# Moving a corner of the first weight split and the denominator product from VectorE to GpSimd in a fused mLSTM and two-MLP kernel

## Chip, cores and metric

The kernel runs on one core of a Trainium2 chip. The metric is the device time of one execution in microseconds (us); the time quoted for a kernel is the median of its runs.

## What is computed

Three stages in float32. First an mLSTM recurrence over 768 steps for 2 batches and 8 heads of 40 features, with input, forget and output gates. Its output, 1536 tokens of 320 features, goes through a gated MLP (two input matrices of 320x1536, an output matrix of 1536x320) and then through a SiLU MLP (320x2048 and 2048x320).

```python
for t in range(S):
    m_new = np.maximum(f_gate[:, :, t] + m, i_gate[:, :, t])
    f_stab, i_stab = np.exp(f_gate[:, :, t] + m - m_new), np.exp(i_gate[:, :, t] - m_new)
    C = f_stab * C + i_stab * outer(v, k)
    n = f_stab * n + i_stab * k
    y[:, :, t] = sigmoid(o_gate[:, :, t]) * (C @ q) / np.maximum(np.abs(n @ q), 1.0)
x = y.transpose(0, 2, 1, 3).reshape(B * S, H * D)
x = (x @ w_a) * (x @ w_b) @ w_out
h = x @ w_in
out = (h * (1.0 / (1.0 + np.exp(-h)))) @ w_out2
```

## The kernel before

**Units.** The recurrence is computed in chunks of 128 steps. A unit u (0 to 11) is one chunk of one batch, so 128 tokens. Of each unit TensorE makes the scores (`s_u`), the values (`y_u` from `vx_u` and `e_u`), the part carried over from earlier chunks (`y_u` from `cn_u`) and the update of the state (`ups_u`). VectorE scans the decays into `e_u` (line 396), multiplies the scores by them (line 425), joins the values (474, 476) and makes the unit's output `x_u` in `outputs()`: the absolute value of the denominator, its maximum with 1, the reciprocal `dn_u`, the product y times `dn_u` (line 486) and the product with the output gate (line 488). The sigmoid of the output gate stands in place in the third part of `kvo_u`, the tile that holds k, v and o of the unit; two such tiles alternate. `x_u` is transposed on TensorE (`px_u`, line 515) and stored as a high and a low part in `xring` (ScalarE line 518, VectorE line 231).

**Weights.** The first MLP has 12 blocks j of 128 hidden features. `load_w1` brings each as two raw tiles. `split_w1(j, 1)` and `split_w1(j, 0)` turn a raw tile into a tile `cvt_j` (ScalarE lines 237 and 241, VectorE line 245), round it into the high part of `w_j` (ScalarE lines 257, 264, 266) and subtract to get the low part (`rest`, line 231). Two `cvt` tiles alternate between all these parts, so the first step of a part waits until the part two before it has been read for the last time. The last 64 of the 320 input features share one 128-row slab: their high part stands in one half of the partitions and their low part in the other half, so the subtraction of the low part (64x128, twice a block) writes to other partitions than it reads.

**Stages.** The first MLP works in passes over blocks of 2 or 3 units and ranges of j (`PASSES`): `m0` is units 0 and 1 with j 0 to 4, `m1` units 2 and 3, and so on; in a pass, `a` and `b` are the two products of the first layer (`h`, line 537), `c` the second layer (`acc`, lines 546 to 548). The second MLP begins inside the last pass (`n0`) and then runs alone.

**Order.** All the work up to the first block of the second MLP is cut into steps, and the table `ORDER` names which step is recorded next; each engine carries out its instructions in that order. `warm` is 8 small matmuls on the tile `idle` whose result nothing reads (line 367). All DMAs of the kernel are issued from the queue of SyncE (SP), in the order of the table too; an issue that waits for a buffer holds back the ones behind it.

Of the kernel before, what the change touches and what calls it, by code (L numbers as in the profile page):

```python
# [48 lines left out]
u4.out u4.upd w6.b m1.1.a lw8 u5.d0 w7.a u5.sk u4.out w7.a m1.0.b u3.upd u9.f1 m1.1.b l6.k l5.t w7.b m0.4.b m1.2.a
w7.a m1.2.b l6.t m1.0.b m1.1.b u4.adv w7.b w7.b m1.0.b u5.s0 w8.b w7.a m0.4.c u5.s1 u5.w0 m1.2.a m1.3.a u5.sv u3.adv  # L50
u5.w1 u5.v0 u5.f1 l6.q u5.car w8.b w8.b m1.1.b u4.d1 m1.2.b m1.0.b u5.v1 l6.k l7.k m1.3.a m1.3.b w8.b u5.comb u5.sk
u4.px w7.b l6.e lw9 m0.end m0.end m1.4.a u5.sig w8.a m1.1.b w8.a l7.k l6.k u7.f1 lw10 l7.k w8.b u5.out m1.0.c w7.b
u5.out u5.upd u4.xs l7.e m1.1.c m1.3.b u5.px m1.2.b w9.a m1.4.a u5.xs w7.b m1.4.b w8.a u5.adv m1.3.b w8.b l7.q m1.2.b
m1.2.c w8.a u6.s1 u6.s0 u4.xs w8.a u5.xs m2.0.a u6.car m2.1.a w9.b m1.3.b m1.4.b m1.3.c m2.0.a u0.comb m2.0.b u6.sv
l8.q m1.4.b m2.1.b u6.d0 m1.4.b w9.a w9.a m2.0.b m2.2.a u6.sk u6.sig m1.4.c m2.1.a u6.w0 m1.end m2.2.a m1.end m2.2.b
u10.sk m2.1.b w9.a m2.0.b u6.v0 w9.a m2.1.b m2.0.b u6.w1 u7.s0 m2.3.a u6.sk m2.1.b m2.0.c l8.k l8.k m2.4.a w9.b l8.k
m2.3.b w10.b m2.2.b u7.d0 m2.2.b m2.4.b w9.b m2.3.a lw11 l8.e u6.v1 l7.t m2.3.b m2.4.a m2.1.c u7.sk m3.5.a u7.w0
m2.2.b l8.t l9.e m2.3.b m3.5.a u7.s1 m2.3.b m2.4.b m2.4.b u6.comb m3.5.b m2.2.c m3.6.a m4.5.a u9.d1 m3.6.a m2.3.c
m3.6.b m3.5.b w10.b l9.t u8.s1 u8.f0 u6.out l9.q m3.7.a w10.b u6.upd w9.b m4.5.a m2.4.b u8.d0 w9.b m3.7.a m3.7.b l9.k
l9.k u11.f0 m3.6.b m2.4.c m3.5.b m3.7.b m4.6.a m4.5.b m2.end w10.a m3.6.b u11.sk w10.a u7.sk u7.sv m3.5.b u8.sk u8.s0  # L60
u7.w1 m3.5.c w10.b u2.f1 u6.adv m2.end u5.d1 m4.6.b w9.b m4.6.a m3.6.b m4.5.b m4.7.a m3.7.b m3.7.b m4.7.b l10.q m4.6.b
m5.5.a m3.6.c m3.7.c u6.out u8.sv m4.7.a m5.5.a u7.v0 w10.b u8.w1 u7.v1 m4.5.b w11.b u7.car m4.7.b w11.b m3.end m3.end
w10.b m4.6.b m4.5.b m5.6.a m4.7.b w10.a l9.k m4.5.c m5.5.b m4.6.b u8.w0 u7.sig m4.6.c w11.b u7.comb m4.7.b m5.6.a
m4.7.c u7.out m5.5.b m5.6.b m5.6.b m5.7.a u8.car m5.5.b m6.8.a w10.a m6.8.b m5.7.a u7.out u7.d1 w11.b u8.v0 u8.sk
m6.9.a m6.8.a m4.end u8.sig m6.8.b m4.end m5.7.b w11.a m5.6.b m5.5.b u7.upd m5.7.b l10.k m5.5.c m5.7.b w10.a m5.6.b
m6.9.a u9.d0 u8.v1 m6.8.b m5.6.c w11.a m6.10.a l10.k w11.b m6.10.a m6.9.b u8.comb m6.8.b w11.a w11.b m6.10.b m5.7.b
u9.sk m6.9.b w11.a l10.e m7.8.a u6.px m5.7.c u9.f0 w11.a m6.9.b u7.adv m6.10.b u9.sk m7.8.a l10.k m6.10.b m6.11.a
m6.8.c m6.9.b m6.10.b l10.t u8.upd m6.11.a u8.out u9.s1 m7.8.b m6.11.b m6.9.c u6.xs m5.end u9.sig m5.end u6.xs m6.11.b
u8.out m6.10.c m7.9.a m7.8.b u9.s0 l11.k u8.adv m7.9.b m7.10.a u8.px m6.11.b m6.11.b m7.8.b m7.8.b m7.10.b u7.px l11.k
u9.sv m7.9.a m7.10.a m7.11.a u9.w1 m6.11.c m7.11.b u10.sv m7.9.b m7.11.a m7.10.b m8.8.a u10.s0 l11.q m7.8.c u10.d0  # L70
u7.xs l11.t m7.9.b m7.9.b m6.end m8.8.b m7.10.b u9.w0 m8.9.a u6.f0 m8.8.a m7.9.c m8.9.b m7.11.b m8.9.a u7.xs m6.end
m8.8.b u8.xs u9.car u8.xs u9.upd u9.v0 m7.10.b m8.10.a u10.w0 l11.e m7.11.b m8.9.b m7.10.c u4.f0 m7.11.b m7.11.c l11.k
m8.9.b m8.8.b u9.v1 u9.adv u10.d1 m7.end u10.car u10.s1 m8.11.a u9.comb m8.10.b m8.10.a u10.w1 m8.11.b m9.0.a u9.out
# [735 lines left out]
```

## Time and profile before

| | us |
|---|---|
| median of 3 runs | 477.45 (473.94 to 478.1) |
| the profiled execution | 473.43 |
| its span, from the first to the last instruction | 471.7 |
| TensorE busy in the span | 458.2 (97%) |
| VectorE busy | 210.6 (45%) |
| ScalarE busy | 208.1 (44%) |
| GpSimd busy | 169.4 (36%) |

The profiled execution has its own time, 1.73 us more than its span. Every duration further down is from that execution, so a sum made of them stands against 473.43. The mean granted TensorE clock was 0.994 of full speed. In the table of stages each engine has its busy time and, in brackets, its number of instructions. PEld is TensorE's weight load, DVE VectorE, ACT ScalarE, POOL GpSimd.

### The profile page before, as it was taken

To read this page: it belongs to the slowest core of one execution; us is meant where nothing else is said; L and a number is where in the kernel's file an instruction comes from. 1 tells how busy PE (TensorE), PEld (TensorE's weight loads), DVE (VectorE), ACT (ScalarE), POOL (GpSimd) and SP (SyncE) were. 2 spreads that over 40 slices of the span, in tenths; PEclk is the share of its full clock that TensorE was granted. 3 is DMA by queue.
4 is the path that set the end of the run, shared out by engine and by line. 5 is a ranking of instruction groups with operands and counts; after the bars stand their busy time and mean duration, and the time that the engine had idled before them with its cause. 6 is when DMAs were issued, how large, how long until landed. Compare 5 with 4: busy or idle time off the path is not lost.

```text
span 471.7 us, 7975 instructions
## 1 busy us (share of the span) xinstructions
PE 458.2 (97%) x3095; PEld 438.3 (93%) x3095; DVE 210.6 (45%) x406; ACT 208.1 (44%) x461; POOL 169.4 (36%) x187
## 2 busy tenths in 40 slices
PE   6988999999999999999999999999999999999996
PEld 5988999999999999999999999998999998999995
DVE  7799997746547554523444574375420000000000
ACT  3676466444443321222355546565444233343333
POOL 2654635553344313112122223334342433433332
...
GB/s 242 227 230 247 309 137 245 187 79 92 21 26 154 49 18 91 63 2 61 17 166 65 107 127 75 123 75 109 1 0 57 0 1 1 1 56 1 0 1 56
DMA packets 14289, 41.52 MB, mean 88 GB/s; under 512 B 1772, under 2 KB 6284, under 8 KB 14252
## 3 DMA queue, kind: packets, MB, share of 16 engines
...
q14 instruction: 13, 0.11, 0.1%
...
## 4 chain that ended last, share of the span: by engine, by line
PE 87%; DVE 7%; ACT 2%; issue 2%; DMA 1%; SPq 0%; ACTq 0%; DVEq 0%
PE h L537 46%; PE acc L546 8%; PE acc L547 8%; PE acc L548 8%; PE s_u L418 3%; PE y_u L431 3%; PE cw L546 2%; PE cw L547 2%; PE cw L548 2%; DVE e_u L396 2%; PE px_u L515 2%; PE y_u L441 1%; PE fb_u L387 1%; DVE cvt_j L245 1%; PE ups_u L451 1%
## 5 line engine op out<-in xcount | busy, mean ns | idle before, releaser
L537 PE MATMUL h<-xring,w_j 128*128 128x256 f32 (+2 forms) x1088 | 184.6, 318 | 0.5 <-DVE g L588 0.5
L537 PEld LDWEIGHTS h<-xring,w_j 128*128 128x128 f32 x1088 | 162.3, 189 | 5.0 <-DVE g L588 0.7
L231 POOL TENSOR_TENSOR g<-g,g 128x256 fp32r<-128x256 f32 (+1 forms) x60 | 56.0, 935 | 147.0 <-ACT g L557 141.4
L231 POOL TENSOR_TENSOR g2w<-gw,g2w 128x512 fp32r<-128x512 f32 x48 | 63.3, 1319 | 110.9 <-ACT g2w L557 108.8
L537 PE MATMUL h<-xeven,w_j 128*128 128x512 f32 x256 | 64.0, 392 | 0.0
L537 PEld LDWEIGHTS h<-xeven,w_j 128*128 128x128 f32 x256 | 47.0, 188 | 8.5
L588 DVE TENSOR_TENSOR g<-a,h 128x256 f32<-128x256 f32 (+1 forms) x60 | 28.1, 471 | 58.2 <-POOL g L231 28.0
L594 ACT ACTIVATE gw<-h 128x512 f32<-128x512 f32 x48 | 28.7, 597 | 57.2 <-PE h L537 54.6
L557 ACT CAST g<-g 128x256 fp32r<-128x256 f32 (+1 forms) x60 | 26.8, 449 | 60.8 <-PE acc L548 32.3
L231 DVE TENSOR_TENSOR w_j<-cvt_j,w_j 64x128 fp32r<-64x128 f32 (+2 forms) x72 | 34.5, 479 | 29.4 <-ACT w_j L286 17.1
L581 ACT ACTIVATE a<-h 128x256 f32<-128x256 f32 (+1 forms) x60 | 25.5, 425 | 48.8 <-PE h L537 39.8
L546 PE MATMUL acc<-w_j,g2w 128*128 128x320 f32 x144 | 44.2, 310 | 0.0
L547 PE MATMUL acc<-w_j,g2w 128*128 128x320 f32 x144 | 44.0, 309 | 0.0
L557 ACT CAST g2w<-gw 128x512 fp32r<-128x512 f32 x48 | 29.8, 622 | 30.5 <-PE acc L548 30.1
L548 PE MATMUL acc<-w_j,g2w 128*128 128x320 f32 x144 | 39.9, 311 | 0.0
L546 PE MATMUL acc<-w_j,g 128*128 128x320 f32 x120 | 38.5, 321 | 0.7 <-DVE x L616 0.3
L548 PE MATMUL acc<-w_j,g 128*128 128x320 f32 x120 | 37.1, 309 | 0.0
L547 PE MATMUL acc<-w_j,g 128*128 128x320 f32 x120 | 37.0, 308 | 0.0
L231 POOL TENSOR_TENSOR w_j<-cvt_j,w_j 128x320 fp32r<-128x320 f32 (+1 forms) x24 | 26.3, 1100 | 26.6 <-ACT w_j L257 15.1
L546 PEld LDWEIGHTS acc<-w_j,g2w 128*128 128x128 f32 x144 | 27.1, 188 | 1.4
L547 PEld LDWEIGHTS acc<-w_j,g2w 128*128 128x128 f32 x144 | 27.1, 188 | 1.4
L548 PEld LDWEIGHTS acc<-w_j,g2w 128*128 128x128 f32 x144 | 26.4, 188 | 0.6
(109 smaller groups left out, 667.1 us busy)
## 6 DMA issues: line engine op xcount, KB each, us to landing
...
```

The source lines that it names most:

```text
L231: return eng.tensor_tensor(out=out_, in0=x, in1=hi.bitcast(F32), op=ALU.subtract)
L396: nc.vector.tensor_tensor_scan(out=e, data0=f, data1=ident8[:, h].rearrange("p h t -> p (h t)"), initial=0.0, op0=ALU.mult, op1=ALU.add)
L418: nc.tensor.matmul(out=s[:, i], lhsT=kz[u % 2][:, j, g], rhs=un["q", u][:, g], start=True, stop=True)
L431: nc.tensor.matmul(out=T["y1"][:, h], lhsT=un["e", u][:, h], rhs=T["v"][:, h], start=True, stop=True)
L537: nc.tensor.matmul(out=po, lhsT=w[:, wi * P:(wi + 1) * P], rhs=xt[:, :, xi], start=(n == 0), stop=(n == len(pairs) - 1))
L546: nc.tensor.matmul(out=o, lhsT=hi, rhs=w[:, off:off + DM], start=first, stop=False)
L547: nc.tensor.matmul(out=o, lhsT=hi, rhs=w[:, off + DM:off + 2 * DM], start=False, stop=False)
L548: nc.tensor.matmul(out=o, lhsT=lo, rhs=w[:, off:off + DM], start=False, stop=last)
L557: nc.scalar.copy(out=t[:, 0], in_=g)
L581: nc.scalar.activation(out=a[j], in_=pa, func=ACT.Copy, scale=WS ** -2)
L588: nc.vector.tensor_tensor(out=g, in0=a.pop(j), in1=pb, op=ALU.mult)
L594: nc.scalar.activation(out=g, in_=ph, func=ACT.Silu, scale=1 / WS)
```

## The change

Three edits.

1. In `split_w1(j, 1)` the low part of the last 64 features is no longer subtracted by VectorE into the other half of the partitions. GpSimd subtracts it, in two halves of 64x128, into a new tile `tl` (two of them alternate) in the partitions in which it reads, and two DMAs on SP's queue carry the halves into their place in `w_j`.
2. In `outputs()` VectorE no longer multiplies y by `dn_u`. GpSimd multiplies the output gate by `dn_u` in place, and VectorE's last product takes that.
3. `ORDER` is another table throughout: the steps of the new pieces are in it (59 more entries in all), one `warm` is gone, and nearly all others stand at other places.

```diff
@@ ORDER
-const l1.q const u3.f0 li const const zeros lf run0 u3.f1 warm lw0 run0 l0.t u6.d1 warm expf0 l0.k l0.k run1 run1
+lf const zeros zeros const const const li l0.q warm const run0 lw0 l0.k l0.k l0.t run0 run0 warm expf0 run1 sel run1
...
@@ split_w1, part 1
         yield
+        tl = cvt.tile([P, P], F32R, tag="tl", name=f"tl_j{j}")
         for p, q_, s_ in halves[::-1]:
-            rest(nc.vector, t[q_, s_], c[p, 0:P], t[p, s_])
-        yield
+            rest(nc.gpsimd, tl[p], c[p, 0:P], t[p, s_])
+            yield
+        for p, q_, s_ in halves[::-1]:
+            nc.sync.dma_start(out=t[q_, s_].bitcast(F32), in_=tl[p].bitcast(F32))
+            yield
         rest(nc.gpsimd, t[:, 10 * P + DM:], c[:, P:], t[:, 10 * P:10 * P + DM])
@@ outputs
             nc.vector.reciprocal(out=dn, in_=d)
-            nc.vector.tensor_tensor(out=y, in0=y, in1=dn.to_broadcast([P, H, D]), op=ALU.mult)
+            yield
+            od = un["o", u]
+            nc.gpsimd.tensor_tensor(out=od, in0=od, in1=dn.to_broadcast([P, H, D]), op=ALU.mult)
+            yield
             T["x"] = x = at.tile([P, 3 * P], F32, tag="x", name=f"x_u{u}")
             nc.vector.tensor_tensor(out=x[:, 0:DM].rearrange("p (h d) -> p h d", d=D), in0=y,
-                                    in1=un["o", u], op=ALU.mult)
+                                    in1=od, op=ALU.mult)
             yield
```

What the table does on three engines is shown at the start of the program, where units 0 and 1 are brought to their outputs. Lines 231, 245, 488 and 515 of before are lines 234, 248, 498 and 525 of the kernel after; line 486 has no counterpart, line 495 is the new product on GpSimd and line 276 the new DMA.

VectorE before, from the conversion of the block j 3 to the output of unit 1 (`cvt_j3` is that block's converted tile, `x_u1` the output):

```order
L245 SCALAR_TENSOR_TENSOR cvt_j3_432<-cvt_j3_432,cw_444 128x448
L396 SCALAR_TENSOR_TENSOR e_u2_437<-e_u2_437,ident8_93 128x1024
L360 COPY gb_97<-pgb_474 120x36
L245 SCALAR_TENSOR_TENSOR cvt_j3_446<-cvt_j3_446,cw_464 128x512
L231 TENSOR_TENSOR w1_j3_431<-cvt_j3_432,w1_j3_431 64x128 x2
L482 TENSOR_SCALAR y1_u1_425<-y1_u1_425 128x8
L483 TENSOR_SCALAR y1_u1_425<-y1_u1_425 128x8
L485 RECIPROCAL dn_u1_508<-y1_u1_425 128x8
L486 TENSOR_TENSOR y1_u1_425<-y1_u1_425,dn_u1_508 128x8x40
L488 TENSOR_TENSOR x_u1_511<-y1_u1_425,kvo_u1_254 128x320
```

VectorE after, the same place:

```order
L403 SCALAR_TENSOR_TENSOR e_u2_386<-e_u2_386,ident8_93 128x1024
L248 SCALAR_TENSOR_TENSOR cvt_j3_447<-cvt_j3_447,cw_461 128x448
L489 TENSOR_SCALAR y1_u1_453<-y1_u1_453 128x8
L490 TENSOR_SCALAR y1_u1_453<-y1_u1_453 128x8
L492 RECIPROCAL dn_u1_492<-y1_u1_453 128x8
L498 TENSOR_TENSOR x_u1_503<-y1_u1_453,kvo_u1_291 128x320
L367 COPY gb_97<-pgb_474 120x36
L248 SCALAR_TENSOR_TENSOR cvt_j3_499<-cvt_j3_499,cw_518 128x512
L432 TENSOR_TENSOR e_u2_386<-s_u2_509,e_u2_386 128x512
```

The two rows of line 231 and the two of line 486 are gone from ahead of `x_u1` (of line 231 there were 8 instructions in all up to there), and the second conversion of j 3 (`cvt_j3_446`, now `cvt_j3_499`) stands behind it.

TensorE before, from the transposes of unit 1 to the first products of the first MLP (`h`; `ups` is the update of the state, `y2` the carried part):

```order
L515 MATMUL px1_u1_539<-ident_90,x_u1_511 128x128 x3
L451 MATMUL ups_u1_543<-vx_u1_372,kvo_u1_254 120x123 x3
L441 MATMUL y2_u2_552<-cn_u0_411,qT_u2_462 128x123 x2
L441 MATMUL y2_u2_552<-cn_u0_411,qT_u2_462 128x82
L537 MATMUL h_568<-xring_91,w1_j0_184 128x256 x8
L537 MATMUL h_581<-xring_91,w1_j0_184 128x256 x8
L431 MATMUL y1_u2_593<-vx_u2_560,e_u2_437 128x41 x4
L537 MATMUL h_599<-xring_91,w1_j1_276 128x256 x8
L451 MATMUL ups_u2_608<-vx_u2_560,kvo_u2_514 120x123 x3
```

TensorE after, from the last of the 8 warm matmuls that stand behind the transposes of unit 1 (`s_u2` is the second half of the scores of unit 2):

```order
L374 LDWEIGHTS idb_92
L374 MATMUL idle_113<-idb_92 128x128
L458 MATMUL ups_u1_547<-vx_u1_326,kvo_u1_291 120x123 x3
L425 MATMUL s_u2_557<-qT_u2_342,kz0_108 128x128 x4
L547 MATMUL h_569<-xring_91,w1_j0_209 128x256 x8
L547 MATMUL h_583<-xring_91,w1_j0_209 128x256 x8
L438 MATMUL y1_u2_597<-vx_u2_530,e_u2_386 128x41 x8
L547 MATMUL h_611<-xring_91,w1_j1_273 128x256 x8
L448 MATMUL y2_u2_624<-cn_u0_443,qT_u2_342 128x123 x2
L448 MATMUL y2_u2_624<-cn_u0_443,qT_u2_342 128x82
L547 MATMUL h_637<-xring_91,w1_j1_273 128x256 x8
```

The 8 warm matmuls and the second half of the scores now stand ahead of the first `h`, and the carried part `y2_u2` stands behind three of them; before, the scores of unit 2 stood ahead of `px1_u1`.

GpSimd before, around the low parts of the blocks j 2 and j 3 and up to unit 2:

```order
L231 TENSOR_TENSOR w1_j2_337<-cvt_j2_338,w1_j2_337 128x320
L231 TENSOR_TENSOR w1_j2_337<-cvt_j2_382,w1_j2_337 128x512
L231 TENSOR_TENSOR w1_j3_431<-cvt_j3_432,w1_j3_431 128x320
L231 TENSOR_TENSOR w1_j3_431<-cvt_j3_446,w1_j3_431 128x512
L401 COPY vx_u2_560<-isg_96 128x8
L402 TENSOR_TENSOR vx_u2_560<-kvo_u2_514,isg_96 128x8x40
```

GpSimd after, the same place (`dn_u0` and `dn_u1` are the reciprocals of units 0 and 1):

```order
L234 TENSOR_TENSOR tl_j2_441<-cvt_j2_354,w1_j2_353 64x128
L495 TENSOR_TENSOR kvo_u0_145<-kvo_u0_145,dn_u0_401 128x320
L234 TENSOR_TENSOR tl_j2_441<-cvt_j2_354,w1_j2_353 64x128
L417 TENSOR_TENSOR kvo_u1_291<-kvo_u1_291,ec_u1_344 128x320
L662 COPY scratch_110<-ident_90 16x120
L234 TENSOR_TENSOR w1_j2_353<-cvt_j2_354,w1_j2_353 128x320
L234 TENSOR_TENSOR w1_j2_353<-cvt_j2_384,w1_j2_353 128x512
L495 TENSOR_TENSOR kvo_u1_291<-kvo_u1_291,dn_u1_492 128x320
L234 TENSOR_TENSOR tl_j3_501<-cvt_j3_447,w1_j3_446 64x128 x2
L408 COPY vx_u2_530<-isg_96 128x8
L409 TENSOR_TENSOR vx_u2_530<-kvo_u2_408,isg_96 128x8x40
L234 TENSOR_TENSOR w1_j3_446<-cvt_j3_447,w1_j3_446 128x320
```

The products with `dn_u0` and `dn_u1` and the halves in `tl` now stand between the low parts of the weights; that of `dn_u1` is directly behind the 128x512 low part of j 2.

SP's queue before, from the load of the raw block j 3:

```order
L206 DMA raw1_j3_363<-in_w1_dram 128x1024
L206 DMA raw1_j3_365<-in_w1_dram 128x896
L196 DMA e_u2_437<-fsd_98 128x1024
L184 DMA kz0_108<-in_k_cols_dram 40x384
L174 DMA qT_u2_462<-in_q_cols_dram 120x384
L206 DMA raw1_j4_492<-in_w1_dram 128x1024
L206 DMA raw1_j4_494<-in_w1_dram 128x896
L190 DMA kvo_u2_514<-in_kvo_dram 128x960
L196 DMA e_u3_529<-fsd_98 128x1024
```

SP's queue after, from the first move of j 1 to the load of the decays of unit 3:

```order
L276 DMA w1_j1_273<-tl_j1_340 64x128 x2
L199 DMA e_u2_386<-fsd_98 128x1024
L193 DMA kvo_u2_408<-in_kvo_dram 128x960
L187 DMA kz0_108<-in_k_cols_dram 40x384
L187 DMA kz1_109<-in_k_cols_dram 40x384
L276 DMA w1_j2_353<-tl_j2_441 64x128
L187 DMA kz0_108<-in_k_cols_dram 40x384
L276 DMA w1_j2_353<-tl_j2_441 64x128
L209 DMA raw1_j4_495<-in_w1_dram 128x1024
L209 DMA raw1_j4_497<-in_w1_dram 128x896
L187 DMA kz1_109<-in_k_cols_dram 40x384
L199 DMA e_u3_533<-fsd_98 128x1024
```

The load of the raw block j 4 now stands behind the load of `kvo_u2` and behind the moves of j 2; before, it stood ahead of `kvo_u2`.

## Rows read from the trace of the kernel before

**Rows 1.** Stages: their length, busy time by engine, clock, DMA share, GB/s.

```profile
20.00:30.00 10.00, 8.50 (x75) 8.25 (x73) 9.46 (x19) 7.39 (x18) 6.65 (x12) 0.83 0.83 227
...
30.00:40.00 10.00, 8.81 (x90) 8.50 (x90) 8.67 (x18) 6.95 (x16) 5.40 (x6) 1.00 0.78 270
...
150.00:200.00 50.00, 49.96 (x377) 49.73 (x378) 25.45 (x58) 11.95 (x31) 11.82 (x19) 1.00 0.17 53
...
450.00:471.70 21.70, 17.43 (x103) 15.92 (x101) 0.00 (x0) 7.17 (x14) 6.47 (x5) 0.96 0.09 30
```

**Rows 2.** What TensorE waited for: total us, times, longest us.

```profile
PE px_u L515 <- DVE x_u L488: 2.3, 2, 1.2
...
PE pg L346 <- DVE scratch L337: 1.5, 1, 1.5
```

**Rows 3.** Timeline, VectorE: start, us, instruction, [idle before, releaser].

```profile
12.96 0.17 DVE L349 COPY isg<-pg 128x16 f32<-128x16 f32 x1 [2.04 <-PE pg L346]
...
34.30 0.68 DVE L245 SCALAR_TENSOR_TENSOR cvt_j<-cvt_j,cw 128x512 uint32<-128x512 uint32 x1
...
35.01 0.58 DVE L231 TENSOR_TENSOR w_j<-cvt_j,w_j 64x128 fp32r<-64x128 f32 x2
...
36.16 0.50 DVE L486 TENSOR_TENSOR y_u<-y_u,dn_u 128x320 f32<-128x320 f32 x1
...
36.70 0.49 DVE L488 TENSOR_TENSOR x_u<-y_u,kvo_u 128x320 f32<-128x320 f32 x1
```

**Rows 4.** Timeline, TensorE, around the start of the first MLP.

```profile
26.26 2.08 PE L418 MATMUL s_u<-qT_u,kz 120*128 120x128 f32 x8
...
34.11 2.03 PE L418 MATMUL s_u<-qT_u,kz 120*128 120x128 f32 x16
...
37.33 0.52 PE L515 MATMUL px_u<-ident,x_u 128*128 128x128 f32 x3 [1.19 <-DVE x_u L488]
...
38.32 0.80 PE L441 MATMUL y_u<-cn_u,qT_u 120*128 120x123 f32 x6
...
38.91 2.15 PE L537 MATMUL h<-xring,w_j 128*128 128x256 f32 x16
...
59.17 0.61 PE L515 MATMUL px_u<-ident,x_u 128*128 128x128 f32 x3 [1.10 <-DVE x_u L488]
```

**Rows 5.** Groups by line and shape: xcount | busy us, mean ns.

```profile
L231 POOL TENSOR_TENSOR w_j<-cvt_j,w_j 128x512 fp32r<-128x512 f32 x12 | 15.4, 1282 | 15.1 <-ACT w_j L257 15.1
...
L231 POOL TENSOR_TENSOR w_j<-cvt_j,w_j 128x320 fp32r<-128x320 f32 x12 | 11.0, 917 | 11.5 <-ACT w_j L264 11.5
...
L231 POOL TENSOR_TENSOR g<-g,g 128x256 fp32r<-128x256 f32 x36 | 30.3, 845 | 69.4 <-ACT g L557 65.6 <-PE acc L548 3.8
...
L402 POOL TENSOR_TENSOR vx_u<-kvo_u,isg 128x320 f32<-128x320 f32 x12 | 8.7, 724 | 0.0
...
L652 POOL COPY scratch<-ident 16x120 f32<-16x120 f32 x6 | 1.5, 274 | 0.0
...
L367 PE MATMUL idle<-idb 128*128 128x128 bf16 x112 | 10.1, 259 | 3.1 <-DVE idb L634 3.1
```

**Rows 6.** What ScalarE waited for at the first step of a conversion.

```profile
ACT cvt_j L237 <- POOL w_j L231: 3.5, 7, 1.4
```

**Rows 7.** Timeline, VectorE scan beside a GpSimd copy; that copy's range of ns.

```profile
54.09 3.39 DVE L396 TENSOR_TENSOR_SCAN e_u<-e_u,ident 128x1024 f32<-128x1024 f32 x1
...
55.27 2.20 POOL L401 COPY vx_u<-isg 128x8 f32<-128x8 f32 x1
...
L401 POOL COPY vx_u<-isg x12: 193/198/2196, 13.2 to 187.8; 128x8 f32<-128x8 f32 x12
```

**Rows 8.** SP's queue, two loads; the one load of the chain of waits.

```profile
25.08 3.77 SPq L206 DMA_DIRECT2D raw_j<-in_w_dram  x2
...
28.96 0.36 SPq L190 DMA_DIRECT2D kvo_u<-in_kvo_dram  x1
...
1.70 2.85 DMA scratch<-in_f_gate_dram
```

More of the change, by code (lines that the diff above doesn't have):

```diff
@@ L49 @@
[L49 to L73, printed above, removed]
@@ new lines @@
+u4.out u3.adv m0.4.b u4.out u5.s1 u5.d0 m1.2.a m1.0.b u4.adv w7.a m0.4.b w7.b m0.4.c u5.sk l6.t m1.1.b m1.0.b u5.sig
+u5.w0 m1.2.b u5.car w7.b m0.end u5.sv w7.b u5.v0 m0.end u5.w1 m1.1.b u5.v1 w7.b u4.out u5.comb m1.2.a m1.0.b w8.b l6.e
+u4.px m1.3.a w8.b m1.0.c u5.out u6.d1 u5.d1 u4.xs m1.1.b u5.out m1.3.a m1.2.b l6.k u5.out w8.b u5.out m1.3.b w7.b
+u5.px w8.b m1.4.a l7.k u4.xs w7.b lw9 u5.xs m1.3.b w7.b m1.1.c m1.2.b u5.xs m1.2.b w8.a u5.sk m2.0.a u5.upd l6.q
+m1.4.a u6.sig m2.1.a l7.k l7.e w8.a m2.0.a m1.4.b w8.b w8.a w8.b m1.3.b w8.b u6.s1 m2.1.a u6.d0 m1.2.c m1.3.b w9.a
@@ new lines @@
+u8.out m7.9.b u9.s0 m6.11.b m6.10.c u8.out m7.8.b m6.11.c m7.9.b m7.10.a u8.upd m7.10.a u10.s0 l10.t u9.sv m8.8.a
+m7.8.b u6.xs m6.end u9.w1 m7.10.b m7.9.b l11.k u8.out u9.w0 m7.11.a u8.px m6.end u9.v0 m7.11.b m8.8.b l11.k l11.e
+m7.9.b m7.8.b u9.sig u8.adv m8.8.a u10.d0 m7.10.b m7.8.c l11.q u10.f0 m7.11.a m7.11.b m7.11.b m7.10.b u8.xs m7.9.c
+l11.k m7.10.b u7.out m7.11.b u9.v1 m8.9.a u9.car m8.9.b m8.9.a u7.px u10.w0 m8.10.a u8.xs m7.10.c m8.8.b u10.sv
+u9.comb u9.out m8.11.a u9.upd m8.9.b u9.out u9.out u7.xs u11.d0 m8.11.a m7.11.c l11.t m8.10.b u11.s0 m8.10.a m8.8.b
@@ new lines @@
+u10.s1 m8.8.b u10.sig u7.xs m8.9.b m8.11.b m8.10.b u10.v0 m8.10.b m9.0.a m7.end m8.9.b u9.adv m7.end m8.10.b m9.0.b
+m9.0.a m8.11.b m8.11.b u10.w1 u11.w0 m8.8.c m8.11.b u10.car u10.v1 m9.1.a m9.1.a m8.9.c m8.10.c m9.1.b u10.comb
+m8.11.c u10.out u10.out m9.0.b m9.2.a m9.2.b m9.1.b m9.2.a u11.sig m8.end u10.out u11.s1 m9.0.b m9.1.b u11.sv m9.2.b
+m9.0.b m8.end u10.out u11.v0 m9.3.a m9.0.c m9.1.b u10.adv u9.out m9.2.b m9.1.c u11.w1 m9.3.a u11.v1 u11.car u9.px
+m9.3.b u11.comb m9.4.a u9.f0 m9.2.b u10.px u10.xs m9.2.c m9.4.a u11.out m9.4.b m9.3.b m9.5.a m9.3.b u9.xs u11.out
@@ new lines @@
+u2.d1 n0.4.b n0.3.c p10 n0.4.c n0.6.b p14 p11 n0.5.b p14 n0.7.b p14 n0.8.b p11 p11 n0.5.c n0.7.b n0.6.c n0.8.b p11
+n0.9.b n0.7.b p14 p14 p13 p14 t7 n0.7.c n0.10.b n0.9.b p13 n0.10.b p13 n0.8.b p11 p13 p11 n0.8.c n0.10.b n0.11.b
+n0.11.b n0.9.b p15 n0.12.b u9.d1 n0.12.b n0.9.c n0.13.b t7 t5 u3.f0 n0.11.b u8.f0 n0.10.c p15 p15 n0.12.b n0.13.b p15
+n0.14.b n0.11.c p13 n0.14.b n0.13.b n0.15.b n0.12.c p13 n0.14.b n0.13.c p15 n0.15.b n0.14.c t5 p15 n0.15.b n0.15.c
+n0.end n0.end n0.end n0.end n0.end n0.end n0.end n0.end
```

84 lines of the change are left out of this document (46 added, 38 removed).

## The prediction

> **What bounds the kernel now.** I read the table of stages first. From 150 to 200 us TensorE is busy 49.96 of 50 us [rows 1], and the stretches up to 450 us read the same way: there TensorE sets the time, and neither VectorE (25.45 of 50) nor GpSimd (11.82) is near its limit. The last 21.7 us hold 17.4 us of TensorE, the rest being the closing output, which the change does not touch. Over the span TensorE is busy 458.2 of 471.7 us, so all its idle time is 13.5 us, 4.3 of it in that last stretch. What is left to win lies at the start. From 20 to 30 us TensorE is busy 8.50 of 10 at a granted clock of 0.83, from 30 to 40 us 8.81, while VectorE is at 9.46 and 8.67 and GpSimd at 6.65 and 5.40 [rows 1]. So in the first 40 us VectorE is the engine that is waited for. The list of TensorE's waits says the same: 2.3 us in two waits for `x_u`, 1.5 us for a gate scan [rows 2]. The two waits for `x_u` stand in the timeline: 1.19 us before the transposes of unit 1 at 37.33, after which the first product `h` starts at 38.91, and 1.10 us before those at 59.17 [rows 4]. Part of TensorE's busy time there is no work either: the 112 idle matmuls take 10.1 us [rows 5].
>
> The end follows from one moment. From the first `h` on TensorE has 432.8 us to go (471.7 less 38.9), nearly all of it work that stays. What the change is worth is how much earlier the first `h` starts, less what of TensorE's work is moved behind it, plus what becomes of later waits.
>
> **The change, part by part.** *What leaves VectorE.* 24 subtractions of 64x128, two of which take 0.58 us, and 12 products with `dn_u` of 0.50 us [rows 3], 7.0 and 6.0 us in all. Behind 150 us that is worth nothing: it lies beside a TensorE that never waits. Ahead of the end of `x_u1` (36.70 plus 0.49, so 37.19) stand 8 of the subtractions (2.3 us) and two of the products (1.0 us), and the conversion of the second half of j 3 (0.68 us) is now behind it. Together 4.0 us less work for VectorE ahead of `x_u1` [rows 3].
>
> *What GpSimd gets.* 24 subtractions of 64x128. No row shows one. The same subtraction takes 1282 ns for 512 and 917 ns for 320 elements a partition, 1.9 ns an element, so 0.55 us for 128; the bounds are 0.27 (a 16x120 copy) and 0.85 us (128x256) [rows 5]. I take 0.55, from the same operation. And 12 products with `dn_u` on 128x320, like the product into `vx_u`: 0.72 us [rows 5]. That is 22 us in all; GpSimd has room for it in every stage, but it sits in a loop. The conversion of a raw tile takes one of two buffers, and ScalarE's first step waits for the last reader of the tile two before it: already 7 such waits on GpSimd, 3.5 us [rows 6]. Before, VectorE's two subtractions (0.58) ran beside GpSimd's 128x320 (0.92). Now GpSimd does both in series, so a round of the loop can become 1.1 us longer. Three rounds (j 0, 1, 2) stand ahead of the last conversion before `x_u1`. The bounds are 0 and 3.3 us. I take two rounds, 2.2 us, since ScalarE does not wait in every round today. So `x_u1` ends 4.0 less 2.2, 1.8 us earlier, at 35.4.
>
> *The DMAs.* 24 moves of 32 KB on SP's queue. None from tile to tile is in the trace; the nearest is the f gate's load, 2.85 us [rows 8]. The bounds are 0 and 2.85 us a block. The moves of j 1 are issued ahead of the loads of unit 2, whose scores TensorE makes before the first `h`, so the weights of the first blocks lie ready and I cost the moves at nothing. If that cover goes, a block is 2.85 us late. What waits behind a move in SP's queue is a rival below.
>
> *What the table moves on TensorE.* Before, transposes, `ups` and the carried part (0.59 us, from 38.32 to 38.91) stand between `x_u1` and the first `h`, 1.72 us from 37.19 to 38.91 [rows 4]. Now 8 idle matmuls (10.1 us by 112 by 8, 0.7 us) and half the scores of unit 2 (half of 2.03, 1.0 us) come in, and the carried part goes behind: 1.1 us more. So the first `h` starts at 35.4 plus 1.72 plus 1.1, 38.2, 0.7 us earlier; the 0.6 us of the carried part are still to be done behind it. Gain 0.1 us.
>
> *TensorE's clock.* In the stretch with the granted clock of 0.83, 8 score matmuls took 2.08 us where 16 took 2.03 later on, so TensorE ran at 1.2 in place of 2.4 GHz, after the 1.5 us wait; the wait of 1.19 us before 37.33 was not followed by that [rows 1, 2, 4]. Which of the two the waits of the new order resemble is open: 0 or 1.0 us for each 8 scores. I take 0.5 us as a loss.
>
> *The second wait.* `x_u2` comes later in TensorE's new order, behind two parts of the second layer, and VectorE has less ahead of it. The 1.10 us before 59.17 go [rows 4]; what is late next is not VectorE any more but TensorE's own queue, as in the stretch from 150 us on.
>
> Sum: minus 0.1, plus 0.5, minus 1.1: 0.7 us less, 472.7 against the profiled execution's own 473.43, a ratio of 0.9985. The median of the three runs is 4.0 us above the profiled execution, and I see nothing in the change that picks one of the two levels, so I put the forecast halfway between: 472.7 plus 2.0, 474.7 us.
>
> *A rule against the change.* One scan of 128x1024 took 3.39 us, and a GpSimd copy that began in it 2.20 us, where the copy's median is 0.198 us [rows 7]. The Trainium skill, "SBUF — State Buffer", section "Who interferes with whom", says that a VectorE instruction with two SBUF inputs holds up a GpSimd instruction that reads SBUF, and that the later of the two blocks fully until the other is done; the trace agrees with it in one copy of 12. By that rule every added instruction of GpSimd that meets a scan pays, not one in 12. By the row one that pays costs 2.0 us more (2.20 less 0.198); if two on the way to `x_u1` do, the gain of 0.7 us turns into a loss of 3.3, 476.7 and on the scale of the forecast 478.7, which the range holds.
>
> **The rivals.** *The start shrinks fully (faster).* No round of the loop grows, the 4.0 us come whole, and VectorE's idle 2.04 us before the first copy of the gates [rows 3] go too, because the table puts the first scan of decays ahead of that copy. For it: VectorE at 9.46 of 10 [rows 1]. Against it: ScalarE's waits for GpSimd [rows 6]. `x_u1` 6.0 us earlier, less 1.1 and 0.6 for TensorE's order, plus the 1.1 of the second wait: 5.4 us, 468.0; on the scale of the forecast 470.0.
>
> *GpSimd paces the start (slower).* `x_u1` needs the product with `dn_u1`, which stands directly behind the 128x512 subtraction of j 2 (1.28 us) and takes 0.72 [rows 5]; VectorE, with the scan of the next unit and all conversions behind `x_u`, waits for it. If this hits both units (4.0 us) and all three rounds grow (3.3), `x_u1` is 3.3 us later than before; with 1.1 and 0.6 from TensorE's order and 1.0 for the clock that is 6.0 us, 479.4; on the scale of the forecast 481.4. It makes the kernel slower from the point at which `x_u1` ends after 36.1 us. For it: GpSimd is already at 6.65 of 10 there [rows 1]. Against it: that is still a third of the time idle.
>
> *SP's queue holds the loads.* The raw block j 4 was issued at 25.08; it now stands behind the load of `kvo_u2`, which waited until 28.96, and five further issues of 0.36 [rows 8]: 5.7 us later. TensorE needs the weights of j 4 only after those of j 0 to j 3, which hides some part of it; the bounds are 0 and 5.7, and halfway, 2.9 us on top of the forecast, makes 475.6, or 477.6 on its scale. Against it: the DMA share of 0.78 [rows 1] leaves room to catch up.
>
> **How the numbers follow.** A measurement here can tell about 1% (4.7 us) from no change. The forecast gets 0.45, the full gain 0.25, GpSimd's pace 0.17, the loads 0.13. The forecast and the loads lie within 1%; the other two lie outside. I take 0.01 from the middle for a wait late in the program that none of the cases names: faster 0.25, same 0.57, slower 0.18. The forecast's own range is 471 to 479; with the outer cases 467 to 481.5.
>
> **What would show it.** `x_u1` ending near 35.4 and the first `h` near 38.2; no wait of TensorE for `x_u2`; TensorE busy 50 of 50 from 150 us on. It is wrong if the first `h` starts before 35 or after 41, if TensorE waits behind 60 us for a `w_j` or for a load, if ScalarE's waits for GpSimd at line 240 stay at 3.5 us in all, or if the product on line 495 is what VectorE waits for in both first units.

## The result and the profile after

The changed kernel takes 471.86 us (median of 4 runs, 470.49 to 471.97), the kernel before beside it 477.77 (4 runs, 473.94 to 479.59): a ratio of 0.9872, with a 95% interval of 0.9834 to 0.991. It is faster by 1.3%, 5.9 us. The profiled execution took 471.92 with a span of 470.2, which is its median, while the profiled execution of before (473.43) lies 4.3 below its median of 477.77. So of the 5.9 us only 1.5 stand between the two profiles. The other 4.4 are told by one number of each execution, TensorE's mean granted clock: of the 62 executions of before that were taken beside the experiments below, 17 had 0.994 or 0.995 and took 473.26 to 475.78, the other 45 had 0.982 to 0.986 and took 476.67 to 480.24. The four of the changed kernel had 0.988 (three, 471.79 to 471.97) and 0.991 (470.49). Against the 17 alone (median 473.95) the changed kernel is 2.1 us faster.

The stages of the changed kernel (length, busy time by engine with the number of instructions, granted clock, DMA share, GB/s), to be read against [rows 1]:

```profile
20.00:30.00 10.00, 9.24 (x95) 8.91 (x94) 6.42 (x13) 6.39 (x13) 6.24 (x14) 0.93 0.67 213
30.00:40.00 10.00, 9.25 (x50) 8.44 (x50) 7.06 (x12) 7.60 (x18) 7.27 (x10) 0.56 0.91 269
150.00:200.00 50.00, 50.00 (x382) 49.97 (x381) 24.86 (x56) 12.51 (x35) 14.87 (x24) 1.00 0.16 53
450.00:470.20 20.20, 15.93 (x93) 14.40 (x91) 0.00 (x0) 6.31 (x12) 5.81 (x5) 0.97 0.09 32
```

VectorE (third busy column) fell from 9.46 and 8.67 to 6.42 and 7.06, TensorE (first) rose from 8.50 and 8.81 to 9.24 and 9.25. But the granted clock from 30 to 40 us is 0.56: TensorE was busier and slower. From 150 us on TensorE is busy throughout, as before. All of TensorE's waits in the whole span (total us, times, longest), against [rows 2]:

```profile
PE idle L374 <- DVE idb L644: 3.3, 1, 3.3
PE y_u L438 <- DVE isg L358: 0.8, 1, 0.8
PE fb_u L394 <- DVE isg L356: 0.6, 1, 0.6
PE px_u L525 <- DVE gb L367: 0.5, 1, 0.5
PE px_u L525 <- DMA kz<-in_k_cols_dram: 0.3, 1, 0.3
PE ups_u L458 <- POOL kvo_u L417: 0.3, 1, 0.3
```

The two waits for `x_u` of 2.3 us are gone, that for unit 2 without a successor. TensorE's timeline up to the first `h` (start, us, instruction, [idle before, releaser]), against [rows 4]:

```profile
26.80 2.17 PE L438 MATMUL y_u<-vx_u,e_u 128*128 128x41 f32 x16 [0.76 <-DVE isg L358]
28.90 2.56 PE L364 MATMUL pgb<-scratch 16*120 16x6 f32 x12
...
32.65 2.10 PE L425 MATMUL s_u<-qT_u,kz 120*128 120x128 f32 x8
35.21 0.87 PE L525 MATMUL px_u<-ident,x_u 128*128 128x128 f32 x3 [0.46 <-DVE gb L367]
35.87 1.06 PE L374 MATMUL idle<-idb 128*128 128x128 bf16 x8
...
38.05 1.42 PE L425 MATMUL s_u<-qT_u,kz 120*128 120x128 f32 x8
39.22 2.24 PE L547 MATMUL h<-xring,w_j 128*128 128x256 f32 x16
```

8 scores take 2.10 us here: from about 28.6 to 38.8 TensorE ran at 1.2 GHz. The first `h` starts at 39.22, later than before (38.91), though `x_u1` is earlier. VectorE's timeline there, against [rows 3] and [rows 7]:

```profile
25.30 0.62 DVE L248 SCALAR_TENSOR_TENSOR cvt_j<-cvt_j,cw 128x448 uint32<-128x448 uint32 x1 [3.02 <-issue]
...
28.85 3.84 DVE L403 TENSOR_TENSOR_SCAN e_u<-e_u,ident 128x1024 f32<-128x1024 f32 x1
...
34.57 0.49 DVE L498 TENSOR_TENSOR x_u<-y_u,kvo_u 128x320 f32<-128x320 f32 x1 [0.84 <-POOL kvo_u L495]
```

`x_u1` ends at 35.06 (before 37.19), and VectorE, the engine that was waited for, now stands idle itself, 3.02 us before a conversion. The new work on GpSimd by group (count, busy us, mean ns, idle before), against [rows 5], then ScalarE's wait for it, against [rows 6]:

```profile
L234 POOL TENSOR_TENSOR w_j<-cvt_j,w_j 128x512 fp32r<-128x512 f32 x12 | 17.1, 1425 | 9.3 <-ACT w_j L260 9.1
L234 POOL TENSOR_TENSOR tl_j<-cvt_j,w_j 64x128 fp32r<-64x128 f32 x24 | 11.8, 490 | 11.5 <-DMA w_j<-tl_j 3.6 <-DMA kz<-in_k_cols_dram 2.9 <-ACT w_j L269 2.4
...
L495 POOL TENSOR_TENSOR kvo_u<-kvo_u,dn_u 128x320 f32<-128x320 f32 x12 | 8.7, 722 | 16.0 <-DVE dn_u L492 15.8
```

```profile
ACT cvt_j L240 <- POOL w_j L234: 13.8, 7, 6.0
```

The two prices were near (490 against 550 ns, 722 against 720). The profile puts 3.6 us of GpSimd's idle time down to a move that had to finish; but the high part that the next subtraction reads was ready only at 27.02 us (ScalarE, line 269), 0.13 us before it began, so the move itself cost no more than that.

### The profile page after: what moved, and what is told of

It is laid out like the page before. It is cut to its first block, busy times and chain, and to the rows that moved or that the text cites. A ratio compares the mean times of both kernels' runs of the same rounds, so it can differ in the third digit from the quotient of the medians.

```text
span 470.2 us, 7986 instructions
## 1 busy us (share of the span) xinstructions
PE 460.1 (98%) x3087; PEld 440.0 (94%) x3087; DVE 198.2 (42%) x370; ACT 207.9 (44%) x461; POOL 186.7 (40%) x223
## 4 chain that ended last, share of the span: by engine, by line
PE 91%; POOL 2%; issue 1%; ACT 1%; DVE 1%; ACTq 0%; POOLq 0%
PE h L547 47%; PE acc L556 8%; PE acc L558 8%; PE acc L557 8%; PE s_u L425 4%; PE y_u L438 4%; PE cw L556 2%; PE cw L557 2%; PE cw L558 2%; PE px_u L525 2%; PE ups_u L458 1%; PE y_u L448 1%; POOL w_j L234 1%; POOL kvo_u L495 0%; POOL kvo_u L417 0%
## 5 line engine op out<-in xcount | busy, mean ns | idle before, releaser
L234 POOL TENSOR_TENSOR g<-g,g 128x256 fp32r<-128x256 f32 (+1 forms) x60 | 54.9, 920 | 125.0 <-ACT g L567 116.8
L547 PE MATMUL h<-xeven,w_j 128*128 128x512 f32 x256 | 65.6, 392 | 0.0
L234 DVE TENSOR_TENSOR w_j<-cvt_j,w_j 128x256 fp32r<-128x256 f32 (+2 forms) x48 | 31.5, 662 | 21.2 <-ACT w_j L288 11.3
L234 POOL TENSOR_TENSOR w_j<-cvt_j,w_j 128x320 fp32r<-128x320 f32 (+1 forms) x24 | 27.4, 1146 | 9.3 <-ACT w_j L260 9.1
L556 PEld LDWEIGHTS acc<-w_j,g2w 128*128 128x128 f32 x144 | 27.1, 188 | 1.6
L557 PEld LDWEIGHTS acc<-w_j,g2w 128*128 128x128 f32 x144 | 27.1, 188 | 1.5
L425 PE MATMUL s_u<-qT_u,kz 120*128 120x128 f32 x192 | 27.8, 292 | 0.1
```

Source lines behind the costliest of these rows:

```text
L234: return eng.tensor_tensor(out=out_, in0=x, in1=hi.bitcast(F32), op=ALU.subtract)
L425: nc.tensor.matmul(out=s[:, i], lhsT=kz[u % 2][:, j, g], rhs=un["q", u][:, g], start=True, stop=True)
L547: nc.tensor.matmul(out=po, lhsT=w[:, wi * P:(wi + 1) * P], rhs=xt[:, :, xi], start=(n == 0), stop=(n == len(pairs) - 1))
L556: nc.tensor.matmul(out=o, lhsT=hi, rhs=w[:, off:off + DM], start=first, stop=False)
L557: nc.tensor.matmul(out=o, lhsT=hi, rhs=w[:, off + DM:off + 2 * DM], start=False, stop=False)
```

## The experiments

All ratios are to the kernel before, executed beside each version on the same chip: e1 to e4 on one chip (median of before 477.74), e5 to e8 (478.01) and e9 to e12 (478.07) on another. A ratio is not the quotient of the two medians. The columns from the clock on are of the profiled execution; the rest is its span less the first `h`.

| kernel | median us (lowest to highest, runs) | ratio (95%) | clock, profiled | `x_u1` ends | first h | rest |
|---|---|---|---|---|---|---|
| before, as on record | 477.77 | 1 | 0.994 | 37.19 | 38.91 | 432.8 |
| e1 before again | 477.90 (474.13 to 480.10, 12) | 1.0006 (0.9971 to 1.004) | 0.994 | 37.43 | 40.03 | 433.7 |
| e8 before, one execution | 478.19 | | 0.985 | 40.09 | 43.62 | 432.9 |
| e5 before, more idle matmuls | 474.42 (473.61 to 474.85, 7) | 0.9933 (0.9903 to 0.9963) | 1.000 | 38.23 | 39.95 | 432.9 |
| e2 table alone | 475.47 (474.38 to 476.34, 12) | 0.9967 (0.9935 to 0.9998) | 0.989 | 35.35 | 41.16 | 432.8 |
| e3 without the first edit | 474.06 (473.62 to 475.58, 12) | 0.9939 (0.991 to 0.9969) | 0.989 | 34.01 | 39.77 | 432.6 |
| e7 without the second edit | 472.43 (471.52 to 476.39, 8) | 0.9906 (0.9868 to 0.9945) | 0.988 | 34.94 | 39.90 | 430.7 |
| changed kernel | 471.86 (470.49 to 471.97, 4) | 0.9872 (0.9834 to 0.991) | 0.988 | 35.06 | 39.22 | 431.0 |
| e9 as e2, more idle matmuls | 474.57 (473.05 to 477.03, 12) | 0.9928 (0.9904 to 0.9951) | 0.989 | 35.37 | 42.54 | 432.8 |
| e10 as e3, more idle matmuls | 473.69 (472.09 to 475.07, 8) | 0.9911 (0.9871 to 0.995) | 0.996 | 33.98 | 37.41 | 435.3 |
| e11 as e7, more idle matmuls | 471.28 (470.21 to 474.37, 6) | 0.9864 (0.9822 to 0.9906) | 1.000 | 34.16 | 37.83 | 431.5 |
| e4 changed, more idle matmuls | 470.17 (469.57 to 471.14, 6) | 0.9859 (0.9814 to 0.9904) | 0.995 | 34.29 | 37.68 | 430.6 |
| e6 as e4, 16 fewer | 470.54 (469.83 to 470.90, 5) | 0.9846 (0.9815 to 0.9877) | 0.994 | 34.98 | 37.61 | 431.1 |
| e12 as e4, 8 moved | 471.31 (470.25 to 472.25, 6) | 0.9854 (0.9817 to 0.9892) | 0.996 | 34.39 | 37.97 | 430.4 |

The first question was whether the two levels of before are its own, and what the table, the edits and the clock are worth each.

**e1**, the kernel before unchanged.

> The kernel before, unchanged, executed again. Theory A (a second level): the kernel before has two levels of time, near 474 and near 478 us, and an execution at the higher one shows a stretch in the first 150 us in which TensorE waits or runs at a granted clock well under 1.00 that the profile at 473.43 does not have. Rival (spread without a place): executions lie anywhere from 474 to 480 us, with the mean granted clock of the span at 0.994 in all of them and no stretch that differs. By theory A the median here is 474 to 478, and longer executions have a lower mean clock.

Measured: five executions with 0.994 or 0.995 at 474.13 to 475.77, seven with 0.982 or 0.985 at 477.87 to 480.10. The kernel before goes from one level to the other on one chip, with the clock.

**e2**, the new table alone.

```diff
-        tl = cvt.tile([P, P], F32R, tag="tl", name=f"tl_j{j}")
...
-            rest(nc.gpsimd, tl[p], c[p, 0:P], t[p, s_])
+            rest(nc.vector, t[q_, s_], c[p, 0:P], t[p, s_])
...
-            nc.sync.dma_start(out=t[q_, s_].bitcast(F32), in_=tl[p].bitcast(F32))
...
-            nc.gpsimd.tensor_tensor(out=od, in0=od, in1=dn.to_broadcast([P, H, D]), op=ALU.mult)
+            nc.vector.tensor_tensor(out=y, in0=y, in1=dn.to_broadcast([P, H, D]), op=ALU.mult)
```

> The new table with both pieces of work back on VectorE: the low part of the last 64 features is subtracted by VectorE into its place (no tile tl, no move), and VectorE multiplies y by the reciprocal at the step where GpSimd multiplied the gate. Theory A (the table does it): VectorE has idle time at the start of the new kernel (3.0 us before 25.3 alone), so 2.3 us of subtractions and 1.0 us of products ahead of the first h are mostly hidden: 471 to 473 us, ratio to before as the changed kernel's within 0.5%. Theory B (the two edits do it): VectorE bounds the start, all 3.3 us show and TensorE waits for x_u2 again: 475 to 478 us.

Measured: 475.47, and no two levels (all 12 between 474.38 and 476.34, at 0.986 to 0.992). The 471 to 473 of theory A fell: what the edits do is not only the clock. The time is theory B's, its way is not: TensorE never waits for `x_u2`, and `x_u1` ends at 35.35, so the table alone brings 1.8 of the 2.1 us by which it is earlier in the changed kernel. What holds TensorE up ahead of the first `h` is the loads of `kz`, a tile that the scores of unit 2 need:

```profile
34.86 0.49 DVE L496 TENSOR_TENSOR x_u<-y_u,kvo_u 128x320 f32<-128x320 f32 x1
...
PE s_u L423 <- DMA kz<-in_k_cols_dram: 2.3, 2, 1.2
```

These loads stand on SP's queue behind that of `kvo_u2`, which waits for the output of unit 0. It was issued at 28.96 in the changed kernel and at 30.43 here, each time less than 0.2 us after that output ended (28.93 and 30.27). So work taken off VectorE ahead of unit 0's output frees a load that TensorE needs. This is read from the rows; no run moved the loads alone.

**e3**, the first edit undone (the upper three pieces of that diff), the product on GpSimd kept.

> The changed kernel with the first edit alone undone: VectorE subtracts the low part of the last 64 features into its place, no tile tl and no moves on SP's queue; the product with the reciprocal stays on GpSimd. Theory A: GpSimd's rounds get 0.9 us shorter and VectorE's 0.6 us longer, which nearly cancels: first h within 1 us of 39.2, time 471 to 472.5 us. Theory B (VectorE bounds the start): 2.3 us more ahead of the first h, 474 us. Theory C (GpSimd paces the start): the first h 1.5 us or more earlier, 470 us or less.

Measured: 474.06, the time that theory B gave. No execution of e3 (473.62 and more) reaches the changed kernel's (471.97 and less): the corner of the weights is worth 2.2 us. But not by theory B's way: `x_u1` ends at 34.01, 1.05 us earlier than with the edit, and the first `h` starts 0.55 us later, not 2.3, again behind a wait for `kz`. The other 1.6 us lie behind the first `h` (432.6 against 431.0).

```profile
33.52 0.49 DVE L496 TENSOR_TENSOR x_u<-y_u,kvo_u 128x320 f32<-128x320 f32 x1
...
34.67 1.23 PE L423 MATMUL s_u<-qT_u,kz 120*128 120x128 f32 x4 [1.30 <-DMA kz<-in_k_cols_dram]
```

**e4**, the changed kernel with 48 more idle matmuls.

```diff
@@ ORDER
-u1.w1 w3.b w2.a u0.out w2.b w2.b u1.v0
+u1.w1 w3.b w2.a u0.out w2.b w2.b warm u1.v0
...
-u0.out pg1 w3.b
+u0.out pg1 warm warm warm w3.b
...
-pg1 u2.s0 u1.px
+pg1 u2.s0 warm warm u1.px
```

> The changed kernel with 48 more idle matmuls on TensorE in the stretch from 26 to 35 us: 8 before the values of unit 1, 24 behind the gate products, 16 behind the first scores of unit 2. The changed kernel's granted clock from 30 to 40 us is 0.56, and the transposes of unit 1, the 8 idle matmuls, the update and the second scores took 4.0 us from 35.21 to the first h at 39.22, where full speed would take 2.5. Theory A (the clock costs): the granted clock of that stretch rises to 0.9 or more, the first h starts 1 to 1.5 us earlier, time 1 to 1.5 us lower. Rival (the idle matmuls are in the way): they delay the transposes of unit 1, the first h starts at 39.2 or later, time the same or up to 2 us higher.

Measured: 470.17, 1.7 below the changed kernel, with the clock at 0.83, short of the 0.9 expected. The stages and the first `h` of e4:

```profile
20.00:30.00 10.00, 10.00 (x114) 9.86 (x113) 7.28 (x14) 6.30 (x13) 6.54 (x13) 1.00 0.59 194
30.00:40.00 10.00, 10.00 (x99) 9.93 (x100) 7.11 (x13) 8.06 (x20) 6.73 (x9) 0.83 0.84 264
...
35.40 0.50 PE L525 MATMUL px_u<-ident,x_u 128*128 128x128 f32 x3
...
37.68 2.24 PE L547 MATMUL h<-xring,w_j 128*128 128x256 f32 x16
```

TensorE shows no idle time from 20 to 40 us. Of the 4.7 us that half clock cost the changed kernel (9.24 times 0.07 plus 9.25 times 0.44) 1.7 are left, and the first `h` comes 1.5 us earlier; the other 1.5 us of the gain went into the added matmuls. From `px` of unit 1 to the first `h`, the same steps took 2.28 us here, at full clock, and 4.01 in the changed kernel.

**e5**, the kernel before with 24 more idle matmuls ahead of the gate transposes and 16 ahead of `px` of unit 1, and **e8**, one execution of the kernel before, for a second profile.

```diff
@@ ORDER
-w2.b u0.v1 w2.a pg1
+w2.b u0.v1 w2.a warm warm warm pg1
...
-w4.b l3.q u2.w1 u1.px
+w4.b l3.q u2.w1 warm warm u1.px
```

> The kernel before, with 24 more idle matmuls ahead of the second gate transposes (where TensorE waits at 24 to 25.5 us) and 16 more ahead of px of unit 1 (where it waits at 36 to 37.3 us). Theory A, the 5.9 us between the medians are mostly the upper of two levels at which the kernel before runs, and that level comes from TensorE's clock falling to 1.2 GHz behind its waits in the first 60 us: with the waits filled no execution lies at a mean clock under 0.994, the upper level is gone, the median is 472.5 to 474.5. Rival B, the upper level has nothing to do with the waits that are filled here: executions still lie at two levels, the median stays at 477 to 478.

> The kernel before once more, for a second profile. If it falls on the upper level (mean clock under 0.99, 477 to 480 us), the rows of the first 60 us show at least two stretches at half clock, each behind a wait of TensorE, and some 3 us more of them than the profile with 473.43 us; if it falls on the lower one (over 0.993, 473 to 476), it repeats that profile.

Measured: e5 474.42, all seven executions at 0.998 or 1.000 and within 1.3 us: the upper level is gone. e8 fell on the upper level, 478.19 at 0.985. Its waits, stages and first `h`:

```profile
26.16 0.23 PE L346 MATMUL pg<-ident,scratch 16*128 16x16 f32 x1 [0.70 <-DVE scratch L337]
...
28.95 1.90 PE L431 MATMUL y_u<-vx_u,e_u 128*128 128x41 f32 x8 [0.53 <-POOL w_j L231]
...
43.62 2.16 PE L537 MATMUL h<-xring,w_j 128*128 128x256 f32 x16
```

```profile
20.00:30.00 10.00, 8.77 (x94) 8.41 (x94) 9.37 (x17) 7.10 (x18) 6.87 (x11) 0.94 0.77 235
30.00:40.00 10.00, 10.00 (x60) 9.72 (x60) 7.02 (x15) 4.93 (x11) 5.35 (x6) 0.50 0.40 147
40.00:50.00 10.00, 10.00 (x80) 9.98 (x78) 7.60 (x13) 5.74 (x15) 0.92 (x2) 0.88 0.67 230
```

Here before runs at half clock from about 28.8 to 42.4 without a break, where the profile on record has it for a quarter as long, behind 26 us. Half clock cost 6.7 us of TensorE (8.77 times 0.06, 10 times 0.50, 10 times 0.12) against 1.4 (8.50 times 0.17, [rows 1]); the first `h` is 4.7 us later, and the rest of the program the same to 0.1 us. One expectation for e8 missed: it is one stretch, not two, behind two short waits instead of one of 1.5 us. And the waits alone do not decide it. The profile of e1, an execution of the lower level (475.42), has the same two waits, and its clock stays at 1.00 until 38 us:

```profile
25.81 0.23 PE L346 MATMUL pg<-ident,scratch 16*128 16x16 f32 x1 [0.71 <-DVE scratch L337]
...
28.61 1.06 PE L431 MATMUL y_u<-vx_u,e_u 128*128 128x41 f32 x8 [0.53 <-POOL w_j L231]
```

What sends one execution to the upper level and not another stays open.

In e5 the same stages, and the wait that it kept, read:

```profile
20.00:30.00 10.00, 9.96 (x123) 9.55 (x122) 9.05 (x17) 7.21 (x18) 7.14 (x11) 1.00 0.76 221
30.00:40.00 10.00, 8.84 (x99) 8.53 (x98) 8.98 (x20) 6.83 (x17) 5.39 (x6) 1.00 0.84 288
...
38.37 0.52 PE L515 MATMUL px_u<-ident,x_u 128*128 128x128 f32 x3 [1.16 <-DVE x_u L488]
```

The two short waits are gone. With the clock at 1.00 throughout VectorE is again at 9.05 and 8.98, and the wait for `x_u1` of [rows 4] is back to its length: clock held, the start of before is bound by VectorE.

**e6**, e4 with 16 idle matmuls taken out: 8 of those behind the first scores of unit 2, and the 8 behind the transposes of unit 1 (the expectation names the place of these wrongly).

> The changed kernel with more idle matmuls as before, but 16 fewer of them: 8 fewer behind the first scores of unit 2, and none of the 8 that stood behind the first products of unit 2. If these 16 only cost their own time (some 0.1 us each, 1.4 us in all) and the clock holds without them, first h comes 0.5 to 0.9 us earlier than 37.68 and the time is 469.3 to 469.8. If they hold the clock, a stretch of half clock comes back between 30 and 40 us and the time is 470.5 to 472.

Measured: 470.54, with the same stretch of half clock, about 30 to 33 us, and 0.7 us of idle time between 30 and 40 us; the first `h` gains 0.07. From the end of `x_u1` to the first `h` it is 2.6 us instead of 3.4, so the 16 did stand in the way; but `x_u1` itself came 0.7 later in this profile, as it had in the changed kernel. Neither expectation fits whole.

**e7**, the changed kernel with the second edit alone undone (the last piece of the diff of e2).

> The changed kernel with its second edit alone undone: VectorE again multiplies y by the denominators, twice in the start (0.50 us each). Theory B, each edit has a worth of its own: 472.6 to 473.6, x_u of unit 1 about 0.5 us later than 34.57, first h 0.5 us later than 39.22. Theory A, only the clock level decides: 471.5 to 472.3 with a mean clock of 0.988 as in the changed kernel.

Measured: 472.43, between the two; the first `h` at 39.90, 0.7 later, as theory B had it, but not by its way: `x_u1` ends at 34.94, 0.1 earlier instead of 0.5 later, and TensorE waits 0.60 us for `kz`. Moving the product to GpSimd did not bring `x_u1` forward. Its executions (471.52 to 476.39) overlap those of the changed kernel: the product's worth of 0.6 us is not told from none.

**e9, e10, e11**: e2, e3 and e7 with the 48 idle matmuls of e4.

> The new table with both pieces of work on VectorE, and the 48 idle matmuls of the best version at the same places. With the clock held, before gave 474.42 and the changed kernel 470.17. Theory A, what the two edits bring is mostly the wait and the clock of the start, which the idle matmuls fill as well: 470.2 to 471.2. Theory B, each edit keeps its worth at full clock (3.6 us together in the medians): 473 to 474.

> The changed kernel with its first edit alone undone (the corner of the weights on VectorE again), and the 48 idle matmuls. Theory A: 470.2 to 471, as with the edit. Theory B, the edit is worth the 2.2 us of the medians at full clock too: 472 to 472.8.

> The changed kernel with its second edit alone undone (y times the denominators on VectorE again), and the 48 idle matmuls. Theory A: 470.0 to 470.7. Theory B, the edit is worth its two multiplications of 0.50 us ahead of x_u of unit 1 or the 0.6 us of the medians: 470.7 to 471.3.

Measured: 474.57, 473.69 and 471.28, beside 470.17 with both edits. Theory A fell for the corner, which with the idle matmuls is worth 3.5 us (473.69 less 470.17; e4 ran on the other chip, and by the ratios it is 2.5) or 3.3 (474.57 less 471.28); no execution of e10 reaches one of e4. Both e9 and e10 lie above theory B's ranges too. The product gives 1.1 and 0.9 here, with executions that overlap. The table is worth nothing there: e9 stands level with e5 (474.42). The execution of e9 that was profiled is the slowest of its twelve, at 0.989; the other eleven lie at 0.991 to 1.000. What TensorE waited for from 60 to 150 us in e10:

```profile
PE h L545 <- DVE xring L234: 0.4, 1, 0.4
PE h L545 <- DVE g L596: 0.4, 1, 0.4
PE y_u L436 <- DVE e_u L430: 0.4, 1, 0.4
PE ups_u L456 <- POOL kvo_u L415: 0.3, 1, 0.3
```

In e11, and in the changed kernel, only the last of the four is left. e10, with the corner on VectorE, has the earliest first `h` of all, 37.41. So the corner brings nothing ahead of the first `h` there; what it saves lies behind.

**e12**, e4 with 8 of the idle matmuls moved ahead of the gate products.

```diff
@@ ORDER
-u0.out pg1 warm warm warm w3.b
+u0.out warm pg1 warm warm w3.b
```

> The changed kernel with the same 48 idle matmuls, but 8 of the 24 behind the second gate products ahead of them, since in the version before the granted clock fell to 1.2 GHz in just these products (30 to 34 us). If the clock then holds at 2.4 GHz: 469.0 to 469.8, 30 to 40 us at 0.95 or more. If it falls all the same or waits for x_u take the place: 470 to 470.5.

Measured: 471.31, and the clock falls all the same:

```profile
28.00:30.00 2.00, 2.00 (x24) 1.90 (x23) 1.74 (x2) 0.10 (x1) 1.87 (x4) 1.00 0.39 68
30.00:32.00 2.00, 2.00 (x19) 1.98 (x20) 2.00 (x2) 1.67 (x4) 0.40 (x1) 0.71 0.71 253
32.00:34.00 2.00, 2.00 (x17) 2.00 (x15) 1.09 (x6) 1.40 (x4) 1.87 (x3) 0.50 0.69 157
```

The rival was right on the clock, though its 470 to 470.5 was missed. e4 has the lowest median, below both kernels; by ratio e6 and e12 stand level with it, and its interval overlaps that of the changed kernel.

The edits under the table of before were not tried, so whether the corner is worth as much in the old order stays open.

## Why the prediction was right and wrong

It forecast 474.7, inside 1%, and gave 0.25 to faster by more; 471.86 lies in the range and outside 1%. Step by step:

| step | forecast | measured |
|---|---|---|
| `x_u1` ends | 35.4 | 35.06 |
| from there to the first `h`, at full clock | 2.8 | 2.4 |
| clock, priced apart | 0.5 | 1.7 |
| from the first `h` to the end | 432.3 (432.8 plus 0.6 less 1.1) | 431.0 |
| the execution's own time | 472.7 | 471.92 |
| level of the median above it | 2.0 | 0 |

(2.8 is 1.72 plus 1.1. Measured, 35.06 to 39.22 is 4.16: 0.15 up to `px`, and 4.01 from there, which took 2.28 in e4 at full clock. So 2.4 at full clock, and 1.7 for the clock.)

*The step that failed* is the last: "I see nothing in the change that picks one of the two levels", and so 2.0 us on top. The level is no property of the measurement. It lies in the first 45 us of the kernel before (e8 against the profile on record) and goes when idle matmuls are put there (e5). The new table has another order there, and its executions no longer part into two groups, in twelve executions without the edits (e2) and in the four with them; the eight of e7 do spread over 4.9 us. By the clock (0.986 to 0.992) most of them lie nearer to the upper level of before than to the lower; but the stretch at half clock costs TensorE 3.9 us in e2 and 4.7 in the changed kernel, against 6.7 in e8. That is 2.0 of the 2.8 us by which the forecast was too high, and it carried the result over the 1%.

*The other 0.8 us.* The term for later waits, 1.1 us, was half of what came. The wait for `x_u2` went, as forecast. Behind the first `h`, versions with the corner on VectorE had 432.6 to 432.9 us to go in profiles that ran at full clock from there on (e1 and e10 did not), versions with it on GpSimd 430.4 to 431.5. The rule "behind 150 us that is worth nothing" holds, but between 60 and 150 us VectorE was still late in three places. Those three are 1.2 us; the rest of the 2 us stands in no row of waits, and stays open.

*GpSimd's side* came out at the forecast size by luck. `x_u1` ended 2.1 us earlier (forecast 1.8, for 4.0 us of work off VectorE less 2.2 for the loop). But e2, with all of that work back on VectorE, has 1.8 of them: the new order did it, which the forecast had credited only with the 0.68 us conversion. With the corner on GpSimd `x_u1` ends later than with it on VectorE (35.06 against 34.01 in e3, 34.29 in e4 against 33.98 in e10), and the place of the product makes 0.1 us (e7, e11). The loop did grow: ScalarE's waits for GpSimd rose from 3.5 to 13.8 us, in the same seven times, and VectorE waited 0.84 us for the product ahead of `x_u1`, though not in unit 0. That did not reach the point, 36.1, from which the slower rival decides.

*The clock* was the right worry with too small a price. Half clock cost 4.7 us of TensorE's time against 1.4 in [rows 1], but TensorE would have waited for part of it. Behind `x_u1` it cost 1.7 us, over the bound of 1.0 that I set for 8 scores.

*SP's queue.* The raw block j 4 was issued later still than feared, and TensorE never waited for a weight: that rival paid nothing. What the queue did hold back were the loads of `kz`, 0.3 us in the changed kernel and 2.3 in e2, which the forecast did not name.

```profile
28.96 0.33 SPq L193 DMA_DIRECT2D kvo_u<-in_kvo_dram  x1
...
31.81 1.01 SPq L209 DMA_DIRECT2D raw_j<-in_w_dram  x2
```

Before, that load was issued at 25.08 [rows 8].

*The rule against the change* bit on the other side. All 12 of GpSimd's copies into `vx_u` took 188 to 210 ns, none was held. But the scan at 28.85, which began while GpSimd was in a 0.71 us product, took 3.84 us against a median of 2.284, and GpSimd's instructions kept their length until 30.54:

```profile
28.78 0.71 POOL L417 TENSOR_TENSOR kvo_u<-kvo_u,ec_u 128x320 f32<-128x320 f32 x1
...
29.69 0.85 POOL L234 TENSOR_TENSOR w_j<-cvt_j,w_j 128x320 fp32r<-128x320 f32 x1
```

The Trainium skill, "SBUF — State Buffer", section "Who interferes with whom", says that order of issue decides which of the two blocks; the trace agrees, with VectorE as the one that paid 1.5 us.
